# Softmax attention with a gated feed-forward on one core: down weights loaded earlier, splits moved and spread, other copied scores

## The chip, the cores and the metric

The kernel runs on one core of a Trainium2 chip. The metric is the device time of one execution, in microseconds (us). The engines named below are TensorE (PE in the profile, its weight loads PEld), VectorE (DVE), ScalarE (ACT), GpSimd (POOL) and SyncE (SP), which issues most of the DMAs from one queue, in order. A bank is one bank of TensorE's accumulation memory, 128 partitions by 512 numbers.

## The reference

Sequence 2048, width 512, all in float32. Cut to what matters:

```
xn = layernorm(x)
q, k, v = split(xn @ wqkv), 32 heads of 16
p = softmax(q @ k^T * 16**-0.5)            # per head, 2048 x 2048
s = (p @ v) @ wo
ffn = (silu(xn @ w_gate) * (xn @ w_up)) @ w_down     # inner width 1792
out = x + s * silu(ffn)
```

## The kernel before

**Precision.** A product that must be near float32 is made of three: operands are split into a high part in a rounded format and a low part (value minus high part), and high by high, high by low and low by high are summed. A split is therefore two DVE instructions, a copy that rounds (CAST in the profile) and a subtraction.

**Opening.** The first 160 us normalise x, project it to q, k and v, and write these to DRAM in the layout that the attention reads. The feed-forward's first gate/up tile is computed there too.

**Attention.** Heads go in 8 groups of 4, queries in 4 batches of 512: 32 units. A unit runs over 16 key tiles of 128. They are cut into blocks (L461 to L475), usually 5, 5 and 6 key tiles; units 27, 29 and 30 have 4 blocks of 4, unit 28 has 6, 6, 4 and unit 31 has 4, 3, 3, 3, 3. There are 101 blocks; `now` is the number of the one being written, and blocks are numbered so below, from 0. For each key tile there are two pairs of heads. A pair's scores take two matmuls of 50 rows that share the array, one per half.

**A block** (`run`, L852) has two stages. In the first, scores and steps of the feed-forward are written in turn; a step (`fill(1)`) is two matmuls of 64 rows (`both`, L184) that share the array and add into the banks `bankx` and `banky`. In the second stage (`values`, L371) TensorE multiplies the block's probabilities by v, 8 matmuls a key tile. TensorE works strictly in the written order.

**Direct and copied scores.** A direct pair ("D") goes into one of two score buffers, and ACT takes the exponential from there (L884), about one microsecond a pair; TensorE can be at most two pairs ahead of ACT. A copied pair goes by halves ("A", then "B") through one spare bank, `acc[1]`; DVE copies each half to SBUF (L896, L902), and ACT takes the exponential of copied pairs at the end of the stage (L908), while TensorE does values. B may be written only when A's copy has been read out. Copied pairs are always the block's last ones. `events` (L477) decides how many pairs are copied and at which step each D, A, B and F (a feed-forward step) stands: `need` is the number of pairs that ACT couldn't take directly in the stage's length, counted in steps; the number copied is that or a limit by length, whichever is less. In the first block nothing is copied, and four of its steps are written ahead of its scores (L855 and following).

**Feed-forward** (`ffn`, L195). Four batches of 512 rows; inner width 1792 is 14 tiles, in two groups of 7. A tile's gate and up products are 24 steps (gate in `bankx`, up in `banky`); then ACT takes a tanh of `bankx`, and DVE makes the hidden values `ga` in two instructions that read both banks (L218, L219). After 7 tiles come four down products of 21 steps, one for each 128 rows. A block takes exactly one of these, 24 or 21 steps; the last ones take the output projection, 9 or 12 steps (`project_out`, L338). "(6,21)" below means a block of 6 key tiles and 21 steps.

**Loads and splits of weights.** `load_gu` (L121) loads a gate/up tile two tiles ahead (`gur`, two buffers), `split_gu` puts its split into `chores`. `load_wd` (L146) loads a tile's down weights into `wdr`, which has one buffer, so that load waits for the split of the tile before; before the change it is issued after the 8th of the tile's 24 products, behind `load_gu`. `split_wd` (L151) puts its split among the chores after the 22nd. `split_hidden` splits `ga` into `hh`.

**Chores.** DVE's splits and the ends of units (`normalise`, `finish`) are kept in a list and written between the copies, where their cost in steps fits before the next copy; `tidy` (L139) writes all that is left, once ahead of the stage's last event and once behind it. DVE executes in that order, so that an instruction that waits holds all behind it. The steps and costs are numbers in the kernel; no scheduler changes the order.

**Output projection.** In the last blocks attention outputs of batches 0 to 2 are loaded from DRAM (`load_out`, L288) and split (`split_out`, L305): all three of a batch at the end of one block (L325). `ready` counts a batch's parts; its projection begins when it has four. `store_out` (L333) multiplies and adds on GpSimd.

Of the kernel before, what the change touches and what calls it, by code (L numbers as in the profile page):

```python
# [28 lines left out]
DT = D // P  # L29
# [21 lines left out]
def tile_block(ctx: ExitStack, tc: tile.TileContext, x, wqkv, wo, w_gate, w_up, w_down, out):  # L51
# [143 lines left out]
    def ffn(b):  # L195
        for grp, part in enumerate(GROUPS):
            nf = part.stop - part.start
            for f in range(nf):
                i = b * NF + part.start + f
                if i + 1 < NB * NF:  # L200
                    split_gu(i + 1)
                if i + 2 < NB * NF:
                    load_gu(i + 2)
                hi, lo = gu.pop(i)
                n = 0
                for c in range(DC):
                    for wt, j in ((hi, 0), (hi, 1), (lo, 0)):
                        both(wt[:, c], fx[:, j, c], n == 0, n == 3 * DC - 1)
                        n += 1
                        if n == 3 * DC - 2 and now >= 0:  # L210
                            split_wd(f, i)
                        if n == DC and i:
                            load_wd(i)
                        if n == 3 * DC:
                            th = one.tile([P, TB], F32, tag="th", name="th")
                            ga = two.tile([P, TB], F32, tag="ga", name="ga")
                            act(th, bankx, AF.Tanh, scale=0.5)  # L217
                            dve.scalar_tensor_tensor(ga, th, 1.0, bankx, op0=ALU.add, op1=ALU.mult)  # L218
                            dve.scalar_tensor_tensor(ga, ga, 0.5, banky, op0=ALU.mult, op1=ALU.mult)  # L219
                            kept.append((f, ga))  # L220
                            if now >= 0:
                                split_hidden()
                            if grp == 1 and f == nf - 1 and b + 1 < NB:
                                load_fx(b + 1, 0)
                                load_fx(b + 1, 1)
                            elif grp == 1 and f == nf - 1:
                                load_wo(0)
                        yield 3 * DC - n
            for t in range(NT):
                n = 0  # L230
                for f in range(nf):
                    for a, w in ((0, 0), (0, 1), (1, 0)):
                        both(hh[:, f, a, t * P:(t + 1) * P], wd[:, f, w], n == 0, n == 3 * nf - 1)
                        n += 1
                        if n == 3 * nf and grp == 0:
                            dve.tensor_copy(facc[:, t], bankx)
                            dve.tensor_add(facc[:, t], banky, facc[:, t])
                        elif n == 3 * nf:
                            y = two.tile([P, D], F32, tag="ga", name="y")
                            dve.tensor_add(y, bankx, facc[:, t])  # L240
                            dve.tensor_add(y, banky, y)
                            after.append(partial(store_gate, y, b * TB + t * P))
                            if b == NB - 1:
                                after.append(partial(next_out, t))
                        yield 3 * nf - n
# [56 lines left out]

    ready = [0] * NB

    def split_out(b):  # L305
        for c in range(DT - 1):
            split_o(lhs[b, c], parts_o[b, c])
            ready[b] += 1

    def out_steps():  # L310
        if now == early:
# [11 lines left out]
            load_gate()  # L323

    def out_splits():  # L325
        if now in (early, early + 1):
            split_out(now - early)
        if now == opened[units - 2] + 1:
            split_out(2)
        if now - opened[units - 1] - 2 in range(EARLY):  # L330
            gate_rest(now - opened[units - 1] - 2)

# [127 lines left out]
    for u in range(units):  # L460
        opened.append(len(blocks))  # L461
        if u == units - 1:
            ns = [4, 3, 3, 3, 3]
        elif u in FINE:
            ns = [4] * 4
        elif u == units - 4:
            ns = [6, 6, 4]
        else:
            ns = [5] * 3
            far = sizes[len(blocks):len(blocks) + 3]  # L470
            ns[far.index(max(far)) if far[1] < max(far) else 1] = 6
        kt = 0
        for n in ns:
            blocks.append((u, kt, n))
            kt += n  # L475

    def events(n, f):  # L477
        length = 2 * n + f
        need = 2 * n - max(2, (10 * length + 46) // 40)
        copied = max(0, min(need, (2 * length - 5) // 22)) if now else 0  # L480
        direct = 2 * n - copied
        gap = max(4, min(5, (length - 8) / max(1, direct - 2)))
        marks = [(0, "D"), (1, "D")] + [(7 + gap * i, "D") for i in range(direct - 2)]
        marks += [(3 + max(5.6, (length - 5) / (2 * copied)) * i, "AB"[i % 2]) for i in range(2 * copied)]
        marks.sort()
        out = []
        at = left = 0
# [426 lines left out]
    for now, (u, first, n) in enumerate(blocks):  # L914
        g, b = divmod(u, NB)
        if first == 0 and 0 < u < units - 1:
            load_q(u + 1)
            load_shift(u + 1)
        if now == 2 or first == 0 and 0 < g < NG - 1 and b == 0:
            load_k(g + 1, 0)  # L920
            load_v(g + 1, 0)
        run(u, first, n)
# [93 lines left out]
```

## Time and profile before

| | us |
|---|---|
| median of 3 runs | 1434.6 (1433.69 to 1435.59) |
| the profiled execution, its own time | 1435.62 |
| its span on the core | 1433.8 |
| TensorE busy | 1409.6 (98%) |
| ScalarE busy | 1080.5 (75%) |
| VectorE busy | 734.7 (51%) |
| GpSimd busy | 89.9 (6%) |
| mean granted TensorE clock | 0.996 |

How to read it: a busy TensorE is one with a matmul in flight, and matmuls overlap, so 98% says that it seldom stands still, and not that nothing can be shortened. The chain of waits follows the work that ended last back through the program; its rows name a line, a start and a duration. In it "PE acc L375" is a run of value matmuls (x40 for a block of 5 key tiles, x48 for 6, x32 for 4, x24 for 3), so that the distance from the end of one such row to the end of the next is the length of a block. A wait is put down to the instruction that ended it.

### The profile page before, as it was taken

How to read it: one execution, taken by the hardware profiler on the slowest of the kernel's cores; microseconds unless marked ns; L12 is line 12 of the kernel's file. 1: busy time of each engine (PE TensorE's matmuls, PEld its weight loads, DVE VectorE, ACT ScalarE, POOL GpSimd, SP SyncE). 2: the span in 40 equal slices, each digit the busy share in tenths (PEclk: the TensorE clock that was granted, in tenths of full speed). 3: DMA queues.
4: the chain of work that ended last, by engine and by line, in shares of the span. 5: the costliest groups of instructions: out<-in, count | busy, mean ns of one | idle time of the engine just before them, and what ended most of it. 6: DMA issues, size and time to landing. Idle time of an engine off the chain costs nothing.

```text
span 1433.8 us, 27758 instructions
## 1 busy us (share of the span) xinstructions
PE 1409.6 (98%) x11227; PEld 860.7 (60%) x11227; DVE 734.7 (51%) x1251; ACT 1080.5 (75%) x1235; POOL 89.9 (6%) x104
## 2 busy tenths in 40 slices
PE   9999899999999999999999999999999999999998
PEld 7777565566555655566556556665566556554445
DVE  6543355356545553556455535554555355445446
ACT  6733577787788777787888778878887778687775
POOL 4200200000000000000000000000000000001333
PEclk9999999999999999999999999999999999999999
DMA  6768642034543511154514303365224112133323
GB/s 221 264 244 252 165 103 50 13 88 95 115 108 97 134 42 35 47 125 101 134 54 114 83 12 79 82 149 123 71 73 115 35 44 67 59 111 108 115 88 119
DMA packets 126956, 148.17 MB, mean 103 GB/s; under 512 B 12524, under 2 KB 79340, under 8 KB 126052
## 3 DMA queue, kind: packets, MB, share of 16 engines
q1 hardware_dynamic: 121620, 125.79, 34.3%
q0 software_dynamic: 4912, 20.12, 3.8%
q8 instruction: 91, 1.49, 0.4%
q14 instruction: 45, 0.37, 0.1%
q10 hardware_dynamic: 288, 0.39, 0.1%
HBM read 106.68 MB, written 39.58 MB: 102 GB/s over the span
## 4 chain that ended last, share of the span: by engine, by line
PE 91%; ACT 4%; DVE 2%; DMA 1%; issue 1%; SPq 0%; DVEq 0%; ACTq 0%
PE acc L375 30%; PE bankx L186 23%; PE score L868 15%; PE banky L186 9%; PE ps L622 6%; ACT pr L884 4%; PE ps L624 3%; PE acc L868 3%; DMA wdr<-in_B_w_down_dram 1%; PE acc L597 0%; DMA v_d<-vt 0%; DMA wraw<-in_A_wqkv_dram 0%; DVE hh L276 0%; PE ps L653 0%; SPq L98 0%
## 5 line engine op out<-in xcount | busy, mean ns | idle before, releaser
L884 ACT ACTIVATE pr<-score 128x1024 f32<-128x1024 f32 x876 | 823.9, 1030 | 260.5 <-PE score L868 260.0
L375 PE MATMUL acc<-pr,vst 128*17 128x512 f32 x4096 | 460.9, 595 | 0.0
L868 PE MATMUL score<-qst,kst 50*128 50x512 f32 x1752 | 412.1, 420 | 10.8 <-ACT pr L884 10.5
L186 PE MATMUL bankx<-fx,guh 64*128 64x512 f32 x896 | 320.2, 394 | 3.3 <-DVE ga L218 3.2
L186 PE MATMUL banky<-fx,guh 64*128 64x512 f32 x896 | 312.3, 395 | 0.6 <-DVE ga L219 0.6
L375 PEld LDWEIGHTS acc<-pr,vst 128*17 128x17 f32 x4096 | 110.3, 97 | 294.7 <-issue 287.8
L868 PEld LDWEIGHTS score<-qst,kst 50*128 50x128 f32 x1752 | 177.3, 184 | 169.9 <-issue 74.8
L186 PE MATMUL bankx<-wd,hh 64*128 64x512 f32 x672 | 199.2, 392 | 0.0
L186 PE MATMUL banky<-wd,hh 64*128 64x512 f32 x672 | 196.6, 391 | 0.0
L896 DVE COPY pr<-acc 128x512 f32<-128x512 f32 x148 | 102.2, 690 | 176.7 <-PE acc L868 173.7
L186 PEld LDWEIGHTS bankx<-fx,guh 64*128 64x128 f32 x896 | 167.2, 187 | 19.7 <-DVE ga L218 4.0
L186 PE MATMUL bankx<-fx,gul 64*128 64x512 f32 x448 | 176.4, 394 | 0.0
L186 PE MATMUL banky<-fx,gul 64*128 64x512 f32 x448 | 176.2, 393 | 0.0
L186 PEld LDWEIGHTS banky<-fx,guh 64*128 64x128 f32 x896 | 167.2, 187 | 6.2 <-DVE ga L219 1.4
L902 DVE COPY pr<-acc 128x512 f32<-128x512 f32 x148 | 102.2, 691 | 102.5 <-PE acc L868 92.1
L908 ACT ACTIVATE pr<-pr 128x1024 f32<-128x1024 f32 x148 | 153.5, 1083 | 0.0
L186 PEld LDWEIGHTS bankx<-wd,hh 64*128 64x128 f32 x672 | 125.1, 186 | 13.1
L186 PEld LDWEIGHTS banky<-wd,hh 64*128 64x128 f32 x672 | 124.9, 186 | 4.4
L868 PE MATMUL acc<-qst,kst 50*128 50x512 f32 x296 | 118.1, 399 | 1.6 <-DVE pr L896 1.5
L218 DVE SCALAR_TENSOR_TENSOR ga<-th,bankx 128x512 f32<-128x512 f32 x56 | 38.5, 687 | 137.9 <-ACT th L217 137.9
L186 PEld LDWEIGHTS bankx<-fx,gul 64*128 64x128 f32 x448 | 84.3, 188 | 6.9
L186 PEld LDWEIGHTS banky<-fx,gul 64*128 64x128 f32 x448 | 84.1, 188 | 1.6
(171 smaller groups left out, 1302.8 us busy)
## 6 DMA issues: line engine op xcount, KB each, us to landing
gur<-in_B_w_gate_dram SPq DMA_DIRECT2D x56, 256.0 KB
gur<-in_B_w_up_dram SPq DMA_DIRECT2D x56, 256.0 KB
wdr<-in_B_w_down_dram SPq DMA_DIRECT2D x56, 256.0 KB
kst<-k_d SPq DMA_DIRECT2D x192, 64.0 KB
qst<-q_d SPq DMA_DIRECT2D x192, 64.0 KB
fx<-xt_d SPq DMA_DIRECT2D x24, 512.0 KB
q_d<-parts SPq DMA_DIRECT2D x16, 512.0 KB
k_d<-parts SPq DMA_DIRECT2D x16, 512.0 KB
```

Source lines behind the costliest of these rows:

```text
L186: mm(banks[i], lhs[halves[i]], rhs[halves[i]], start=start, stop=stop)
L218: dve.scalar_tensor_tensor(ga, th, 1.0, bankx, op0=ALU.add, op1=ALU.mult)
L375: mm(acc[0][h * 32:h * 32 + DH + 1], v[:, kt % CT, h * (DH + 1):(h + 1) * (DH + 1)], probs[kt, h // 2][:, h % 2], start=kt == 0, stop=kt = ...
L622: mm(ps, w, a[:, c], start=n == 0, stop=n == 3 * DT - 1)
L624: mm(ps, a[:, c, tokens], w, start=n == 0, stop=n == 3 * DT - 1)
L868: mm(bank, k[r, j, kc * P:(kc + 1) * P], q[r, j], start=True, stop=True)
L884: act(probs[kt, j], score[done % 2], AF.Exp, scale=0.25)
L896: dve.tensor_copy(probs[kt, j][:, 0], spare_bank)
L902: dve.tensor_copy(probs[kt, j][:, 1], spare_bank)
L908: act(probs[kt, j], probs[kt, j], AF.Exp, scale=0.25)
```

## The change

Five things are changed.

1. A tile's down weights are loaded at its first product, ahead of `load_gu`, instead of after its 8th.
2. In block 0 the split of the down weights is written behind the two instructions that read the banks, instead of ahead of them.
3. The splits of batches 0 to 2 for the output projection are spread: blocks 87, 88 and 89 end with two each (before: three after 87, three after 88), and blocks 93, 94 and 95 with one each (before: three after 93).
4. Unit 0 is cut into blocks of 4, 6 and 6 key tiles instead of 5, 6 and 5, and the load of the second group's first keys and values moves from block 2 to block 3.
5. The limit on copied pairs is another formula, and copies are placed otherwise. Written out, 162 pairs are copied instead of 148: a third pair in the seven blocks (6,21), which are 7, 19, 40, 52, 73, 85 and 86; a second pair in six of the blocks with 4 key tiles and 12 steps, which are 89, 90, 91, 93, 94 and 95; and one more in block 2, which now has 6 key tiles. Elsewhere the number stays. A and B of a pair are at most 8 steps apart by the formula (before: spread over the stage): in the 29 blocks of 5 key tiles and 24 steps B now stands 10.5 steps into the stage.

The order of one (6,21) block and of one (4,12) block, before and after:

```
(6,21)  DDFAFFFFDFFBDFFFDFAFFDFFFDBFFDFFDDF   ->  DDFAFFFFDBFFDFFAFDFFFBDFFDFAFFDFFBDF
(4,12)  DDFAFFFFDFFBDFFFDFDDF                 ->  DDFAFFFFDBFFDFFAFDFBDF
```

The diff:

```diff
@@ ffn @@
             for f in range(nf):
                 i = b * NF + part.start + f
+                if i:
+                    load_wd(i)
                 if i + 1 < NB * NF:
                     split_gu(i + 1)
...
-                        if n == 3 * DC - 2 and now >= 0:
+                        if n == 3 * DC - 2 and now > 0:
                             split_wd(f, i)
-                        if n == DC and i:
-                            load_wd(i)
                         if n == 3 * DC:
...
                             kept.append((f, ga))
+                            if now == 0:
+                                split_wd(f, i)
                             if now >= 0:
                                 split_hidden()
@@ split_out, out_splits @@
-    def split_out(b):
-        for c in range(DT - 1):
-            split_o(lhs[b, c], parts_o[b, c])
-            ready[b] += 1
+    def split_out(b, c):
+        split_o(lhs[b, c], parts_o[b, c])
+        ready[b] += 1
...
-        if now in (early, early + 1):
-            split_out(now - early)
-        if now == opened[units - 2] + 1:
-            split_out(2)
+        for b, c in {early: ((0, 0), (0, 1)), early + 1: ((0, 2), (1, 0)), early + 2: ((1, 1), (1, 2)),
+                     opened[units - 2] + 1: ((2, 0),), opened[units - 2] + 2: ((2, 1),),
+                     opened[units - 2] + 3: ((2, 2),)}.get(now, ()):
+            split_out(b, c)
@@ blocks @@
             ns = [4, 3, 3, 3, 3]
+        elif u == 0:
+            ns = [4, 6, 6]
@@ events @@
-        copied = max(0, min(need, (2 * length - 5) // 22)) if now else 0
+        fit = 1 if ends and length < 24 else (10 * length + 34) // 112
+        copied = max(0, min(need, fit)) if now else 0
...
-        marks += [(3 + max(5.6, (length - 5) / (2 * copied)) * i, "AB"[i % 2]) for i in range(2 * copied)]
+        marks += [(2.2 + max(5.6, min(8, (length - 5) / (2 * copied))) * i, "AB"[i % 2]) for i in range(2 * copied)]
@@ the loop over blocks @@
-        if now == 2 or first == 0 and 0 < g < NG - 1 and b == 0:
+        if now == 3 or first == 0 and 0 < g < NG - 1 and b == 0:
             load_k(g + 1, 0)
             load_v(g + 1, 0)
```

## The prediction, made before the result was known

> **What bounds the kernel.** I read the page first, then the chain of waits, then the timeline where the chain leaves TensorE.
>
> ```profile
> span 1433.8 us, 27758 instructions
> ...
> PE 91%; ACT 4%; DVE 2%; DMA 1%; issue 1%; SPq 0%; DVEq 0%; ACTq 0%
> ...
> L868 PE MATMUL acc<-qst,kst 50*128 50x512 f32 x296 | 118.1, 399 | 1.6 <-DVE pr L896 1.5
> ```
>
> TensorE carries 91% of the chain, so no edit here shortens its work (the products are the same before and after). What can move is the other 9%: stretches where TensorE waits for a score buffer (ACT), for copies or splits (DVE), or for weights (DMA), and the half-clock stretches that such waits bring. A block is one stage of scores and one of values (program order, from 0). Its length is the distance between two ends of value stages, start plus duration in the chain's rows (start, duration, what):
>
> ```profile
> 83.17 22.39 PE ps L622 x96
> ...
> 657.81 5.28 PE acc L375 x48
> ...
> 683.16 4.42 PE acc L375 x40
> 691.78 0.96 ACT pr L884
> ...
> 696.46 5.27 PE acc L375 x48
> 709.22 4.42 PE acc L375 x40
> 721.14 4.42 PE acc L375 x40
> 734.46 5.28 PE acc L375 x48
> ```
>
> One step (a product, or a pair that shares the array) takes 22.39/96 = 0.233 us; one key tile more costs 5.27 - 4.42 = 0.85 us of values. Block 40 has 6 key tiles and 21 feed-forward steps, (6,21): 701.73 - 687.58 = 14.15; block 41, (5,21), takes 11.91, and block 43, (6,24), 739.74 - 725.56 = 14.18. The odd one is (6,21): three steps fewer than (6,24), the same time. The row at 691.78 says why: ten scores go straight to ACT, and TensorE waits for ACT's pitch.
>
> **The change, part by part.**
>
> *A third copied pair in the seven (6,21) blocks.* Nine direct scores remain. Without the wait a block takes between 11.91 + 0.85 + 2 x 0.233 = 13.23 and 14.18 - 3 x 0.233 = 13.48: a gain of 0.67 to 0.92 us. The cost: two copies more on DVE, 0.69 us each (rows of L896 below), and six half scores through one bank, 5.5 steps = 1.28 us apart, against 0.40 (the half score of the group above) + 0.69 + two hand-overs, estimated at 1.2 us. That just fits, so I take 0.75. Below nothing: if each of the six is 0.2 us late, the gain is gone. ACT does the same number of exponentials, the third copied one beside the 5.3 us of values as the other two now. Six of the seven: 4.5 us. Block 85 starts behind a DVE backlog, and its second half score now comes two steps earlier against the same late copy: 0.2 us. Together 4.7.
>
> *A second copied pair in six of the 12-step blocks (89, 90, 91, 93, 94, 95), splits of the output projection spread.*
>
> ```profile
> 1287.61 5.27 PE acc L375 x48
> ...
> 1309.17 4.92 PE acc L375 x32
> ...
> 1320.14 3.56 PE acc L375 x32
> ...
> 1360.46 1.66 DVE hh L276
> ...
> 1369.58 3.56 PE acc L375 x32
> ...
> 1404.37 2.82 PE acc L375 x24
> 1411.66 2.80 PE acc L375 x24
> ```
>
> Block 89 takes 1323.70 - 1314.09 = 9.6. Block 99 (3 key tiles, 12 steps, one pair copied, no wait for ACT) takes 7.27; one key tile more makes 8.59, so at most 1.01 is to be had. But the written order puts the second pair's halves only 3.5 steps = 0.82 us apart, against the 1.2 above: about 0.35 lost. 0.66 each, for five blocks 3.3. Block 90 gets nothing: two splits of batch 1 now end block 89, where GpSimd starts on the gated output; the split at 1360.46 stood in such a place and took 1.66 us, and two like it would hold the first copy of block 90 by about 0.8 us. In block 94 it is the three splits of batch 2, now one per block, that held the first copy, to 1365.27:
>
> ```profile
> 1365.27 0.68 DVE L896 COPY pr<-acc 128x512 f32<-128x512 f32 x1
> ```
>
> Blocks 93 and 94 together took 1373.14 less 1348.92 + 3.56 (the row of block 92, below), 20.66: 1.5 over two of 9.6. This goes too. Sum 4.8 (bounds 2 and 6.5).
>
> *The splits of batch 0, three after block 87 before, two now.* Blocks 87 and 88 take 1314.09 - 1292.88 = 21.21, 2.0 over twice 9.6. Value stage 88 took 4.92 instead of 3.56 at half clock, which followed a stretch in which TensorE was only 72% busy:
>
> ```profile
> 1348.92 3.56 PE acc L375 x32
> ...
> 1304.00:1308.50 4.50, 3.24 (x22) 1.90 (x20) 3.80 (x8) 4.19 (x6) 0.00 (x0) 1.00 0.98 313
> 1308.50:1311.90 3.40, 3.40 (x20) 0.66 (x20) 2.56 (x5) 2.40 (x3) 0.00 (x0) 0.50 1.04 386
> ```
>
> (columns: stretch, length, then busy of PE, PEld, DVE, ACT and POOL, granted clock, DMA share, GB/s). The rest of the 2.0, 0.65, is a first copy held by the splits, and goes with one split fewer; the 1.36 of half clock goes in perhaps 7 of 10 cases, since block 88 stays bound by ACT. I take 1.6 (0.3 to 2.0).
>
> *Down weights at a tile's first product.* SyncE's queue runs in order; the load moves ahead of the two gate/up loads (gur) of 256 KB each. It still waits for the split of the last tile's weights, and now the gur loads wait behind that: they have a whole block, over 11 us, before their split. Where key rows are loaded, the down weights came too late:
>
> ```profile
> 475.73 4.42 PE acc L375 x40
> ...
> 501.97 5.27 PE acc L375 x48
> ...
> 631.40 4.42 PE acc L375 x40
> ...
> 747.90 4.42 PE acc L375 x40
> ...
> 773.83 5.27 PE acc L375 x48
> 787.32 4.42 PE acc L375 x40
> 796.84 6.70 DMA wdr<-in_B_w_down_dram
> 814.84 5.27 PE acc L375 x48
> ```
>
> A (5,24) and a (6,24) block undisturbed take 779.10 - 752.32 = 26.78 (blocks 45, 46). 48 and 49 take 28.37, 24 and 25 take 27.09, 36 and 37 (to 663.09) 27.27: 1.59, 0.31 and 0.49 over, 2.4. The load comes about 1.3 us earlier and without 512 KB ahead of it, some 3 us in all: it does for nearly all. I take 2.2 (1.5 to 2.4).
>
> *The opening: units of 4, 6, 6 key tiles and the split behind the bank reads.*
>
> ```profile
> 169.98 1.29 DVE L906 TENSOR_TENSOR gul<-gur,guh 128x512 fp32r<-128x512 f32 x2
> 170.13 0.66 SPq L125 DMA_DIRECT2D gur<-in_B_w_gate_dram  x1
> 171.58 0.55 SPq L148 DMA_DIRECT2D wdr<-in_B_w_down_dram  x1
> 176.39 0.43 DVE L906 CAST wd<-wdr 128x512 fp32r<-128x512 f32 x1 [5.12 <-DMA wdr<-in_B_w_down_dram]
> 178.20 0.50 PE L186 MATMUL bankx<-fx,guh 64*128 64x512 f32 x1 [2.82 <-DVE ga L218]
> 178.97 0.43 DVE L906 CAST hh<-ga 128x512 fp32r<-128x512 f32 x1
> 180.64 0.68 DVE L896 COPY pr<-acc 128x512 f32<-128x512 f32 x1
> ...
> 178.70:185.50 6.80, 6.51 (x30) 5.42 (x31) 4.45 (x8) 2.05 (x2) 0.00 (x0) 0.50 0.83 183
> ...
> 203.90 4.42 PE acc L375 x40
> ```
>
> Before: DVE waits for the weights, the reads of the banks queue behind, TensorE stands for 2.82 us and then runs 6.8 us at half clock. After: block 0 begins near 160.2 as before; 8 scores and 24 products are 32 steps, 7.45 us, the values begin near 168.0 and end at 171.6. DVE ends its gate split at 171.27, reads the banks by 172.7 (0.3 us of waiting for TensorE), then waits for the weights. Issued at 170.13 they are there between 173.1 (3 us) and 174.9 (the 4.8 us of before); I take 174.1. The wait is thus not gone: behind it stand the weight split (1.07), the hidden split and the gate cast (178.97 to 180.64, 1.67) and the first copy, which ends at 177.5. TensorE wants that bank again 10.5 steps into block 1, at 174.7: it stands 2.9 us there. I add one half-clock period of 3.4 us, 1.7 lost. Block 1: 0.35 + 36 x 0.233 + 0.2 + 0.3 + 2.9 + 1.7 = 13.8, and 5.3 of values: 190.7. Block 2, now (6,24), ends at 204.9, against 208.32: gain 3.4 (1.0 with late weights and two periods, 6 with early weights and none).
>
> In this case half clock followed a stretch without any long pause (1304 to 1308.5), so I count it after 2.9 us. The Trainium skill, "TensorE: Matmul & The Clock Gate", section "Why this matters for your kernels", says otherwise that only gaps of more than about 3 us between bursts bring half clock; the row at 1308.50 disagrees. By that rule the opening would gain 5.1 and the sum would be 1416.
>
> *Earlier second halves elsewhere* (29 blocks (5,24): 10.5 steps after the start instead of 18) cost nothing as long as DVE has done the first copy; see the last rival. K and V of the second group move a block later, needed nine blocks on: nothing.
>
> **Sum.** 4.7 + 4.8 + 1.6 + 2.2 + 3.4 = 16.7 us. The profiled execution took 1435.6 (span 1433.8 and 1.8 around it), 1.0 above the median of 1434.6; it becomes 1418.9, and the median 1417.9.
>
> **Rivals.** (a) No half clock in the opening: 1416. For it: 2.9 us may fall across two periods of observation; against it, the row at 1308.50. (b) The 13 extra pairs do not pay, because the shared bank's round trip of 1.2 us is longer than I read it: 4.5 and 3.3 fall away, 1425.7. For it: spacings of 1.28 and 0.82 us leave no room. Against it: the rows of copy and half score, 1.09 together. (c) The opening gains nothing, because the weights land late and both periods stay: 1421. (d) Slower: in the 29 (5,24) blocks TensorE comes to the second half before the first copy is done.
>
> ```profile
> 209.47 0.69 DVE L896 COPY pr<-acc 128x512 f32<-128x512 f32 x1
> ```
>
> Block 3 began at 208.32; the copy ended 1.84 us in, TensorE will come at 0.33 + 10.5 x 0.233 = 2.78. DVE would have to be 0.94 us later than here before anything is lost; at 0.58 us lost per block the whole gain is gone, at 0.75 the time is 1440.
>
> **How the numbers follow.** A measurement here tells about 0.2%, 2.9 us, from no change. Forecast 1418: 0.48; (a) 0.15; (b) 0.20; (c) 0.09; (d) 0.08, of which 0.03 within 0.2% and 0.05 slower. So faster 0.92, same 0.03, slower 0.05. The likeliest case alone spans 1413 to 1422; with (a), (b) and (c) the range is 1411 to 1427.
>
> **What would show it.** In the changed profile: (6,21) blocks of about 13.4 us; block 91 near 8.9; blocks 48 and 49 near 26.8 together; in the opening no wait for "ga", but one of the second half score (acc, L868 before) for DVE of 2 to 3 us; first three blocks over by 205. Wrong would be: waits of TensorE for the copies in block after block, or half clock at places that had none.

## The result, and the profile after

The changed kernel takes 1422.2 us (median of 4 runs, 1421.64 to 1426.21) against 1435.1 for the kernel before (4 runs): a ratio of 0.9916, 95% interval 0.9895 to 0.9937. That is 13 us less, where 16.7 were predicted; the time lies 4.2 us above the 1418.0 of the prediction, inside its range and just outside that of its likeliest case. The profiled executions differ by 14.0: 1435.62 before, 1421.64 after (span 1419.9).

From the page of the changed kernel, the span, the shares of the chain by engine, and the group of the half scores that share a bank (busy and mean ns, then the idle time ahead of them):

```profile
span 1419.9 us, 27729 instructions
...
PE 94%; DVE 2%; ACT 2%; DMA 1%; issue 1%; SPq 0%; DVEq 0%; ACTq 0%
...
L872 PE MATMUL acc<-qst,kst 50*128 50x512 f32 x324 | 130.5, 403 | 5.2 <-issue 2.5
```

TensorE carries 94% of the chain instead of 91, and ACT 2% instead of 4. There are 324 half scores instead of 296, and TensorE waits 5.2 us for their bank instead of 1.6; 2.5 of these are one wait in the opening. (The page puts that wait down to "issue", which means that it shows nothing that ended it; the rows of the opening below tell what did.) From the chain of waits of the changed kernel (start, duration, what):

```profile
184.95 5.28 PE acc L376 x48
199.11 5.28 PE acc L376 x48
...
676.64 4.42 PE acc L376 x40
689.11 5.27 PE acc L376 x48
...
780.06 4.42 PE acc L376 x40
...
806.00 5.27 PE acc L376 x48
...
1288.61 3.56 PE acc L376 x32
...
1298.22 3.56 PE acc L376 x32
...
1309.37 1.70 DVE wd L278
1311.07 1.44 DVE wd L277
...
1317.46 3.87 PE acc L376 x32
...
1326.90 3.87 PE acc L376 x32
```

As in the prediction, a block's length is the distance between two ends of value stages. Block 40, (6,21), takes 694.38 - 681.06 = 13.32 (before 14.15). Blocks 48 and 49 take 811.27 - 784.48 = 26.79 together (before 28.37). Block 88 takes 1301.78 - 1292.17 = 9.61 (before 11.62). But block 91, one of the six with a second copied pair, takes 1330.77 - 1321.33 = 9.44, and its value stage is longer, 3.87 instead of 3.56. The two rows of DVE in front are from the splits that end block 89: 1.70 and 1.44 us, and block 90 behind them comes to 10.1.

The table adds up all blocks in this way, profiled execution against profiled execution:

| Term of the sum | predicted | measured | blocks |
|---|---|---|---|
| third copied pair, (6,21) | 4.7 | 4.1 | 7, 19, 40, 52, 73: 0.66 to 0.84 each, 3.7; 85: 0.29; 86: 0.11 |
| second copied pair and spread splits, 12 steps | 4.8 | 1.7 | 89, 91, 93, 95: 0.12 to 0.17 each; 90: -0.52; 94: 1.64 |
| splits of batch 0 | 1.6 | 1.4 | 88: 2.01; 87: -0.61 |
| down weights, later blocks | 2.2 | 2.0 | 25: 0.32; 37: 0.16; 49: 1.55 |
| opening | 3.4 | 3.9 | end of block 2: 204.39, before 208.32 |
| the rest | 0 | 0.8 | 30, 31, 68, 80, 96: 0.18 to 0.29 each; 56: -0.25; the end behind the last block: -0.4 |
| sum | 16.7 | 13.9 | |

In the opening the timeline of the changed kernel shows these instructions (start, duration, engine, what, and in brackets the wait and what ended it):

```profile
174.14 0.43 DVE L910 CAST wd<-wdr 128x512 fp32r<-128x512 f32 x1 [0.68 <-DMA wdr<-in_B_w_down_dram]
...
177.22 0.69 DVE L910 CAST guh<-gur 128x1024 fp32r<-128x1024 f32 x1 [0.86 <-DMA gur<-in_B_w_up_dram]
177.83 0.68 DVE L900 COPY pr<-acc 128x512 f32<-128x512 f32 x1
...
178.61 0.46 PE L872 MATMUL acc<-qst,kst 50*128 50x512 f32 x1 [2.47 <-issue]
```

The weights are there at 174.1, as predicted. TensorE then stands for 2.47 us at the half score that wants the bank of the first copy, which starts at 177.83 and takes 0.68. The rows of these stretches by engine (stretch, length, busy of PE, PEld, DVE, ACT and POOL, granted clock, DMA share, GB/s) show what the wait did to the clock, which is nothing here (where the stretches begin and end is explained under "Half clock after a wait" below):

```profile
173.87:177.28 3.41, 2.24 (x16) 1.56 (x15) 2.21 (x5) 1.51 (x2) 0.00 (x0) 1.00 0.98 196
177.28:180.70 3.42, 2.09 (x18) 2.00 (x20) 3.12 (x5) 1.29 (x2) 0.00 (x0) 1.00 1.02 227
```

### The profile page after: what moved, and what is told of

The parts are those of the page before. It is cut to its first block, busy times and chain, and to the rows that moved or that the text cites. A ratio compares the mean times of both kernels' runs of the same rounds, so it can differ in the third digit from the quotient of the medians.

```text
span 1419.9 us, 27729 instructions
## 1 busy us (share of the span) xinstructions
PE 1403.0 (99%) x11227; PEld 847.5 (60%) x11227; DVE 756.3 (53%) x1279; ACT 1082.0 (76%) x1235; POOL 92.7 (7%) x104
## 4 chain that ended last, share of the span: by engine, by line
PE 94%; DVE 2%; ACT 2%; DMA 1%; issue 1%; SPq 0%; DVEq 0%; ACTq 0%
PE acc L376 30%; PE bankx L186 23%; PE score L872 16%; PE banky L186 10%; PE ps L626 6%; PE acc L872 3%; PE ps L628 3%; ACT pr L888 1%; DVE pr L900 0%; DMA v_d<-vt 0%; PE acc L601 0%; ACT pr L912 0%; DMA wraw<-in_A_wqkv_dram 0%; PE ps L657 0%; PE acc L957 0%
## 5 line engine op out<-in xcount | busy, mean ns | idle before, releaser
L888 ACT ACTIVATE pr<-score 128x1024 f32<-128x1024 f32 x862 | 812.0, 1033 | 244.5 <-PE score L872 243.2
L872 PE MATMUL score<-qst,kst 50*128 50x512 f32 x1724 | 396.1, 417 | 3.2 <-ACT pr L888 3.1
L186 PE MATMUL bankx<-fx,guh 64*128 64x512 f32 x896 | 331.5, 393 | 0.3 <-DVE ga L218 0.2
L186 PE MATMUL banky<-fx,guh 64*128 64x512 f32 x896 | 323.3, 393 | 0.3 <-DVE ga L219 0.3
L872 PEld LDWEIGHTS score<-qst,kst 50*128 50x128 f32 x1724 | 172.5, 184 | 158.6 <-issue 72.3
L900 DVE COPY pr<-acc 128x512 f32<-128x512 f32 x162 | 112.0, 691 | 171.6 <-PE acc L872 167.0
L186 PEld LDWEIGHTS bankx<-fx,guh 64*128 64x128 f32 x896 | 166.4, 186 | 19.9 <-issue 0.9
L912 ACT ACTIVATE pr<-pr 128x1024 f32<-128x1024 f32 x162 | 166.6, 1081 | 0.0
L906 DVE COPY pr<-acc 128x512 f32<-128x512 f32 x162 | 111.9, 691 | 88.4 <-PE acc L872 72.9
L872 PE MATMUL acc<-qst,kst 50*128 50x512 f32 x324 | 130.5, 403 | 5.2 <-issue 2.5
```

Source lines behind the costliest of these rows:

```text
L186: mm(banks[i], lhs[halves[i]], rhs[halves[i]], start=start, stop=stop)
L872: mm(bank, k[r, j, kc * P:(kc + 1) * P], q[r, j], start=True, stop=True)
L888: act(probs[kt, j], score[done % 2], AF.Exp, scale=0.25)
L900: dve.tensor_copy(probs[kt, j][:, 0], spare_bank)
L906: dve.tensor_copy(probs[kt, j][:, 1], spare_bank)
L912: act(probs[kt, j], probs[kt, j], AF.Exp, scale=0.25)
```

## The experiments

Twelve kernels were run. All edits are against the changed kernel, but for the one that starts from the kernel before. Ratios are to the kernel before on the same chip.

| Kernel | median us | ratio and interval |
|---|---|---|
| changed, run again | 1423.23 | 0.9916 (0.9902 to 0.9930) |
| loads late again | 1428.29 | 0.9940 (0.9919 to 0.9960) |
| two copied pairs in (6,21) | 1426.89 | 0.9930 (0.9910 to 0.9951) |
| one copied pair at 12 steps | 1423.81 | 0.9916 (0.9894 to 0.9937) |
| splits together again | 1423.93 | 0.9913 (0.9891 to 0.9934) |
| even distances at 12 steps | 1426.33 | 0.9926 (0.9908 to 0.9943) |
| one exponential left out | 1423.12 | 0.9900 (0.9868 to 0.9933) |
| opening as before, load early | 1420.34 | 0.9880 (0.9862 to 0.9898) |
| block 1's copies late | 1418.42 | 0.9872 (0.9855 to 0.9890) |
| kernel before, load early alone | 1427.96 | 0.9947 (0.9931 to 0.9964) |
| splits of 84 to 87 as chores | 1421.46 | 0.9901 (0.9883 to 0.9918) |
| the last two late edits together | 1415.73 | 0.9866 (0.9850 to 0.9882) |

Runs of the same opening differ by a stretch or two at half clock, each of 3.4 us, so a few tenths in a median decide nothing. The verdicts below rest on the lengths of blocks. Where the opening is the same, blocks that no edit and no half clock touches repeat to within 0.07 us; where an edit shifts all that follows (experiments 2, 7, 8, 9 and 11), a few blocks far from it move by 0.1 to 0.3 us (19, 37, 56 and 68 in experiment 9), which nothing here explains.

**1. The load of the down weights alone, undone.**

```diff
-                if i:
-                    load_wd(i)
...
+                        if n == DC and i:
+                            load_wd(i)
```

> The changed kernel with one part undone: the down weights are loaded after a tile's 8th product again, behind the gate/up loads. Theory: the part was worth what blocks 25, 37 and 49 lost less, 0.3 + 0.2 + 1.6 = 2.0 us, and in the opening the weights land at about 176.4 again instead of 174.1, so that the first copy of block 1 ends 1.0 to 2.3 us later: block 49 back near 15.7 us, the whole 3.0 to 4.3 us slower than the changed kernel. Rival: the load's place does nothing in the opening, because the gate/up tile that then lands earlier (it ended the last 0.9 us of that wait) takes its part: block 1 as in the changed kernel within 0.5 us, the whole 2.0 slower.

From the timeline and the chain of that run:

```profile
177.27 0.43 DVE L910 CAST wd<-wdr 128x512 fp32r<-128x512 f32 x1 [3.91 <-DMA wdr<-in_B_w_down_dram]
```

```profile
202.74 5.27 PE acc L376 x48
```

The weights come 3.1 us later than in the changed kernel (177.27 against 174.14), and block 2 ends at 208.01 instead of 204.39, of which a half-clock stretch at 180.5 is about 1.15. Blocks 25, 37 and 49 are 0.91, 1.06 and 1.16 longer, block 13 0.37. In 25 and 37 the late load costs more in this order than it cost before the change. In all the early load is worth about 6 us by these blocks (2.5 in block 2 without the half clock, 3.5 in the four others), more than both theories had expected. It is the largest part of the change, and more than the 2.2 us at which the prediction booked it; the rest it had booked under the opening.

**2. A third copied pair in (6,21), taken back.**

```diff
+        fit = min(fit, 2)
         copied = max(0, min(need, fit)) if now else 0
```

> The changed kernel with at most two copied pairs in a block, so that the seven (6,21) blocks copy two again. Theory: in blocks 7, 19, 40, 52 and 73 the third pair gained 0.7 to 0.8 us each, in 85 0.3, in 86 0.1, and it cost 0.6 in block 87, because the third copied exponential delays the tanh of the gate behind it, DVE's work that waits for the tanh, and so the next block's first copy. Then 7, 19, 40, 52, 73 return to 14.15, block 87 returns to 9.6, and the whole is 3.4 us slower. Rival: block 87 is slower because the second half of its copied pair stands a step earlier against a copy that is late anyway; then block 87 stays near 10.2 us and the whole is 4.0 us slower.

Blocks 7, 19, 40, 52 and 73 become longer by 0.66, 0.81, 0.81, 0.70 and 0.71: the 0.75 of the prediction. The chain at blocks 85 to 87 of that run:

```profile
1268.27 5.27 PE acc L376 x48
...
1282.42 5.28 PE acc L376 x48
...
1293.91 3.56 PE acc L376 x32
```

Block 86 takes 14.16 and block 87 9.77. In the changed kernel they take 14.03 and 10.21. So the third pair is worth 0.45 in block 85 and 0.12 in 86, and costs 0.43 in block 87: together 0.14. The rival, by which block 87 would have stayed near 10.2, is refuted.

**3. A second copied pair in the blocks of 12 steps, taken back.**

```diff
+        fit = 1 if length < 24 else fit
         copied = max(0, min(need, fit)) if now else 0
```

> The changed kernel with one copied pair in every block of 12 steps or fewer, as before the change. Theory: the second pair is worth next to nothing there, because ACT's eight exponentials follow one another without a break through both stages and the block ends when the last of them and its values are done: blocks 89, 91, 93, 94 and 95 go from 9.44 to 9.60, the whole is slower by 0.8 us at most. Rival: the second pair does remove a wait of 0.9 us and gives it back through its own late half; then without it too blocks are at 9.60, and the two theories part only in the order of the copies, which another run changes. Block 90, where DVE's splits meet GpSimd's product, stays above 9.6 by up to 0.5 us.

From the chain:

```profile
1318.93 3.56 PE acc L376 x32
...
1328.51 3.56 PE acc L376 x32
```

Block 91 takes 9.58 with one copied pair and 9.44 with two; 89, 93, 94 and 95 gain 0.12 to 0.17, and block 90 loses 0.13 by it. Value stages take 3.56 again. The six pairs are thus worth 0.75 - 0.13 = 0.6 in all, where the prediction had 3.3.

**4. One exponential fewer in those blocks.** In blocks 89, 90, 91, 93, 94 and 95 the exponential of the first copied pair is left out; the values are computed from what stands there.

```diff
-        for kt, j in waiting:
+        for kt, j in waiting[1:] if n == 4 and len(waiting) == 2 else waiting:
```

> The changed kernel without the exponential of the first copied pair in the six 12-step blocks with two such pairs (89, 90, 91, 93, 94, 95): the raw scores go on to the values there, so that part of the softmax is left out. Theory: ACT's row of exponentials sets the length, and with one fewer the value stage no longer waits: from 9.44 to about 9.1 us (3.6 of values and the 5.5 of the score stage), 2 us in all. Rival: the spacing of the halves alone makes the extra time and the value stage's extra 0.3 us come from the late last copy on DVE; then the blocks stay near 9.44.

ACT's rows in the timeline of block 91, first in the changed kernel:

```profile
1321.86 5.93 ACT L888 ACTIVATE pr<-score 128x1024 f32<-128x1024 f32 x6 [1.62 <-PE score L872]
...
1327.69 1.99 ACT L912 ACTIVATE pr<-pr 128x1024 f32<-128x1024 f32 x2
```

and then with one left out:

```profile
1321.89 5.91 ACT L888 ACTIVATE pr<-score 128x1024 f32<-128x1024 f32 x6 [2.25 <-PE score L872]
...
1327.70 1.05 ACT L912 ACTIVATE pr<-pr 128x1024 f32<-128x1024 f32 x1
```

In the changed kernel ACT's eight exponentials run without a break from 1321.86 to 1329.68, and the block that began at 1321.33 ends at 1330.77: 0.53 ahead of the row, 7.82 of exponentials, 1.09 of last products behind it. With two of the eight copied instead of one, ACT has the same eight to do. With one left out five of the six blocks become shorter by 0.30 to 0.35 (block 91: 9.10), and another limit comes next; block 90, which the splits hold, stays at 10.13. TensorE's rows of the same block, the two halves of the second copied pair:

```profile
1324.71 0.39 PE L872 MATMUL acc<-qst,kst 50*128 50x512 f32 x1
...
1325.95 0.50 PE L872 MATMUL acc<-qst,kst 50*128 50x512 f32 x1
```

They start 1.24 us apart where the order puts 3.5 steps, 0.82 us, between them: TensorE is held for 0.4. It is held as long in the changed kernel, hidden behind ACT.

**5. The halves of the short blocks closer to even, 4.8 apart by the formula.**

```diff
-        marks += [(2.2 + max(5.6, min(8, (length - 5) / (2 * copied))) * i, "AB"[i % 2]) for i in range(2 * copied)]
+        apart = 4.8 if length < 24 else max(5.6, min(8, (length - 5) / max(1, 2 * copied)))
+        marks += [(2.2 + apart * i, "AB"[i % 2]) for i in range(2 * copied)]
```

> The changed kernel with the copied halves of its short blocks (under 24 steps in all) 4.8 steps apart, so that the two pairs of the 12-step blocks stand 4.5 and 5.5 steps apart by halves instead of 5.5 and 3.5. Rival (the prediction's own): the 3.5 steps cost 0.35 to 0.5 us of TensorE's time a block; then blocks 89, 91, 93, 94 and 95 fall from 9.44 to about 9.1 us and the whole by 1.7 us or more. Theory: ACT's eight exponentials in a row set the length; then the score stage gets shorter, the value stage waits that much longer, and the blocks stay within 0.1 us of 9.44.

The row of ACT in the timeline of block 91 that begins with the third direct score:

```profile
1325.13 3.92 ACT L889 ACTIVATE pr<-score 128x1024 f32<-128x1024 f32 x4 [0.32 <-PE score L873]
```

The blocks became longer, 9.70. TensorE still waits at the second half, and now the third direct score comes late, so that ACT's row has a hole of 0.32: the length follows ACT (9.44 + 0.27). The theory that only the 3.5 steps between two halves hold the block is refuted, since it asked for a shorter one; the other, which asked for no change, missed the hole. Blocks with one copied pair became longer too: 97 to 100 by 0.41 each, 87, 88, 92 and 96 by 0.33 to 0.42. There A and B came closer as well, to 4.5 steps (1.05 us), and B now stands ahead of the third direct score instead of behind it. In block 97 the two halves, and ACT's row from that third score on:

```profile
1381.88 0.39 PE L873 MATMUL acc<-qst,kst 50*128 50x512 f32 x1
...
1383.12 0.50 PE L873 MATMUL acc<-qst,kst 50*128 50x512 f32 x1
...
1383.94 2.85 ACT L889 ACTIVATE pr<-score 128x1024 f32<-128x1024 f32 x3 [0.33 <-PE score L873]
```

The halves start 1.24 us apart, as in experiment 4, and the third direct score waits behind the second half, so that ACT's row has a hole of 0.33; in the changed kernel the five direct exponentials of such a block run without a break. So this is the same loss as in block 91: a score that ACT needs stands behind a half that is held. The hold alone, 1.24 - 4.5 x 0.233 = 0.19, is less than half of the 0.41. The 5.5 steps (1.28 us) of the (6,21) blocks are just enough by the same number.

**6. The splits of a batch together again.**

```diff
-        for b, c in {early: ((0, 0), (0, 1)), early + 1: ((0, 2), (1, 0)), early + 2: ((1, 1), (1, 2)),
-                     opened[units - 2] + 1: ((2, 0),), opened[units - 2] + 2: ((2, 1),),
-                     opened[units - 2] + 3: ((2, 2),)}.get(now, ()):
+        for b, c in {early: ((0, 0), (0, 1), (0, 2)), early + 1: ((1, 0), (1, 1), (1, 2)),
+                     opened[units - 2] + 1: ((2, 0), (2, 1), (2, 2))}.get(now, ()):
```

> The changed kernel with the splits of the output projection as before, three at the end of blocks 87, 88 and 93. Theory: what the spreading moved is undone: block 94 1.5 us longer (near 10.9), block 88 0.65 us longer (near 10.3, and 1.4 more where half clock follows), block 90 0.5 us shorter (near 9.6), the whole 1.7 to 3.0 us slower. Rival: block 94 gained because of its second copied pair and not by the splits; then it stays within 0.3 us of 9.44, and the whole is within 1 us of the changed kernel.

The chain of that run, blocks 92 and 94 and between them the split that holds:

```profile
1337.89 3.56 PE acc L375 x32
...
1349.05 1.66 DVE hh L278
1350.70 1.44 DVE hh L277
...
1358.17 3.87 PE acc L375 x32
```

Blocks 93 and 94 take 20.59, against 18.86 in the changed kernel: the spread is worth 1.7 there, as booked (1.5). Block 88 is 0.64 longer, also as booked (0.65). Block 90 is 0.68 shorter (9.44): the two splits that end block 89 in the changed kernel cost this much, and nothing forces them to stand there.

**7. The opening as before, with the early load kept** (units of 5, 6, 5; the split ahead of the bank reads; keys and values at block 2).

```diff
-        elif u == 0:
-            ns = [4, 6, 6]
...
-                        if n == 3 * DC - 2 and now > 0:
+                        if n == 3 * DC - 2 and now >= 0:
...
-                            if now == 0:
-                                split_wd(f, i)
...
-        if now == 3 or first == 0 and 0 < g < NG - 1 and b == 0:
+        if now == 2 or first == 0 and 0 < g < NG - 1 and b == 0:
```

> The changed kernel with its opening undone (unit 0 in blocks of 5, 6, 5; keys of the second group after block 2; the down weights' split ahead of the bank reads in block 0), but with the down weights still loaded at the first product. Theory: the early load alone did the opening's work; the weights land at about 174.1, DVE reads the banks by 176.7, TensorE stands about 1.2 us there and 0.4 us at the first copy, and block 2 ends near 203 us, 1.4 to 2.5 us ahead of the changed kernel. Rival (the prediction's step): the new order and the smaller first block carry the opening's gain; then block 2 ends near 208 and the whole is 3 to 4 us slower.

From its chain:

```profile
170.59 6.18 PE acc L374 x40
...
185.67 5.27 PE acc L374 x48
199.14 4.42 PE acc L374 x40
```

Block 2 ends at 203.56, 0.83 earlier than in the changed kernel (less than the 1.4 to 2.5 expected), though this run has a half-clock stretch there (at 170.9, granted clock 0.51 from 170.90 to 174.30) and the changed one has none. Block 1 has no wait (14.17).

**8. The early load alone, in the kernel before.** The same move of `load_wd` to the first product, and nothing else.

> The kernel before with one part of the change alone: the down weights loaded at a tile's first product. Theory: this part carries the whole gain of the opening and of the loads between groups: block 2 ends near 202 us (203.6 with a half-clock period) instead of 208.3, blocks 24 and 25, 36 and 37, 48 and 49 take 26.8 us by pairs, and the whole is 7 to 8.5 us faster than the kernel before. Rival: in the opening the early load helps only together with the split behind the bank reads; then block 2 ends near 206 or later and the gain is 2 to 4 us.

From its chain, the value stage of block 2:

```profile
198.79 4.42 PE acc L375 x40
```

One moved load takes 7.7 us (1435.65 to 1427.96): block 2 ends at 203.21 instead of 208.32, and blocks 25, 37 and 49 gain 0.29, 0.48 and 1.59. So the changed kernel's new order of the opening, with the same load, ends 1.2 us later than the old order does.

**9. Block 1's copies later.** The copies of block 1 begin at step 16, and DVE's other work of that block stands behind them.

```diff
-        marks += [(2.2 + max(5.6, min(8, (length - 5) / (2 * copied))) * i, "AB"[i % 2]) for i in range(2 * copied)]
+        start, apart = (16, 5.6) if now == 1 else (2.2, max(5.6, min(8, (length - 5) / max(1, 2 * copied))))
+        marks += [(start + apart * i, "AB"[i % 2]) for i in range(2 * copied)]
...
-            while chores and at < final and (not copying or max(free, t) + chores[0][0] <= copying[0] + 0.5):
+            while chores and at < final and (now != 1 or not copying) and (not copying or max(free, t) + chores[0][0] <= copying[0] + 0.5):
```

> The changed kernel with the two copied pairs of block 1 moved back, the first half to step 16 instead of 3, and DVE's other work of that block behind the copies. Theory: TensorE's 2.7 us wait in block 1 is for the bank whose copy stands behind the waits for the down and gate weights, and half clock follows it by chance of the observation period; with the copies late the wait goes, block 1 falls from 18.3 (19.5 with half clock) to about 15.3 us, the whole is 3.0 us faster, and no run has half clock in the opening. Rival: the wait only moves to the next tile's gate weights, whose split now comes later; then block 2 is longer by what block 1 gains.

From its chain:

```profile
181.35 5.28 PE acc L376 x48
195.51 5.27 PE acc L376 x48
```

Block 1 takes 14.82 instead of 18.32, block 2 is not longer (14.15), and block 2 ends at 200.78. The whole wait of 2.47 us was the place of the first copy in the order, and it does not come back in block 2, as the rival had it; no half clock follows in the profiled run either. Block 1 gains 1.0 more than the wait; DVE's other work was moved too, and the two were not separated.

**10. The splits of blocks 84 to 87 among the chores.** They are no longer written at a block's end, ahead of the next one's first copy, but among the chores, and in blocks 85 to 87 no chore is written ahead of the first copy (`held`).

```diff
-        if t:
-            split_o(lhs[NB - 1, t - 1], plain[t - 1])
-        split_wo(t)
+        chores.append((2, lambda: dve.tensor_copy(fx[:, 0, t], wor[t])))
+        chores.append((3, lambda: dve.tensor_sub(fx[:, 1, t], wor[t], fx[:, 0, t].bitcast(F32))))
...
+            for c in range(DT - 1):
+                hi, lo = lhs[NB - 1, c]
+                chores.append((2, partial(dve.tensor_copy, hi, plain[c])))
+                chores.append((3, partial(dve.tensor_sub, lo, plain[c], hi.bitcast(F32))))
...
+        held = len(copying) if u == units - 4 else -1
...
-            while chores and at < final and (not copying or max(free, t) + chores[0][0] <= copying[0] + 0.5):
+            while chores and at < final and len(copying) != held and (not copying or max(free, t) + chores[0][0] <= copying[0] + 0.5):
```

> The changed kernel with the splits of the last batch's outputs and of the projection's weights (next_out) written among the chores, the outputs' already in block 84, and in blocks 85 to 87 nothing of the chores ahead of the first copy. Theory: the third pair earns little in 85 and 86 and costs in 87 because DVE stands behind the tanh with this work when the first copy is due; without it blocks 85 and 86 fall from 14.46 and 14.03 to 13.3 to 13.5 us and 87 from 10.20 to 9.6, 2.2 us in all. Rival: these blocks are long by ACT alone, which has the tanh besides its exponentials there; then they stay within 0.3 us each.

DVE's rows at the end of block 85 in the changed kernel:

```profile
1267.08 0.69 DVE L191 SCALAR_TENSOR_TENSOR y<-th,y 128x512 f32<-128x512 f32 x1 [2.75 <-ACT th L190]
...
1269.20 0.69 DVE L258 TENSOR_TENSOR fx<-wor,fx 128x512 fp32r<-128x512 f32 x1
1269.81 0.68 DVE L900 COPY pr<-acc 128x512 f32<-128x512 f32 x1
```

The gate's tanh stands behind the copied exponentials on ACT, and with a third of these it comes later; the splits wait behind it, and the first copy of block 86, which began at 1267.93, starts at 1269.81. With the splits among the chores blocks 85, 86 and 87 gain 1.10, 0.67 and 0.60 (13.35, 13.36 and 9.60).

**11. Experiments 9 and 10 together, with one more split moved** from the end of block 89 to that of block 90:

```diff
-        for b, c in {early: ((0, 0), (0, 1)), early + 1: ((0, 2), (1, 0)), early + 2: ((1, 1), (1, 2)),
+        for b, c in {early: ((0, 0), (0, 1)), early + 1: ((0, 2), (1, 0)), early + 2: ((1, 1),), early + 3: ((1, 2),),
```

> The two mendings together, late copies in block 1 and the splits of next_out among the chores, and one split a block in blocks 89 and 90. Theory: the gains add up, 3.5 us in the opening (more where half clock was), 2.2 in blocks 85 to 87 and 0.5 in block 90: 6 us less than the changed kernel, about 1416 where that takes 1422, and no half clock before the end. Rival: work pushed behind the copies comes back as longer blocks later, and the gain is under 4 us.

From its page and chain:

```profile
span 1413.5 us, 27726 instructions
...
PE 96%; ACT 1%; DVE 1%; DMA 1%; issue 0%; SPq 0%; DVEq 0%; ACTq 0%
...
181.40 5.28 PE acc L379 x48
```

1415.7 us (four runs, 1415.27 to 1417.15): 7.5 less than the changed kernel run again, 19.9 less than the kernel before. Block 90 takes 9.44, block 1 14.82, block 85 13.31.

**12. The changed kernel again.**

> The changed kernel itself once more beside the others. Theory: its runs fall into some with half clock in the opening and some without, about 1.2 us apart, by where the observation period lies against the wait of 2.7 us; the granted clock tells them apart. Rival: the spread has another source, and runs of equal clock differ by as much.

Six runs gave 1421.69 to 1428.88, a wider spread than the 1.2 us expected; the two longest, 1425.98 and 1428.88, have the lowest mean clocks, 0.996 and 0.995. In the profiled one, which is the longest, block 1 takes 21.01 instead of 18.32, and two of the stretches by engine are at half clock (a third lies at 10.0 us, long before the attention):

```profile
180.70:187.50 6.80, 6.37 (x30) 5.49 (x32) 2.90 (x5) 3.07 (x3) 0.00 (x0) 0.50 0.98 187
1293.40:1296.80 3.40, 3.22 (x16) 1.00 (x20) 1.83 (x4) 3.01 (x4) 0.00 (x0) 0.50 0.26 60
```

The same program has no such stretch in the profile of the result above, with a wait of 2.47 us where this run has 2.61. Block 87 took 11.67 here, 10.21 there.

## Why the prediction was right, and where it was off

**The third copied pair (4.7, measured 4.1): right.** 0.66 to 0.84 in the five blocks that begin undisturbed, against 0.75, and experiment 2 takes exactly this back. The reading of the odd row, ten direct scores at ACT's pitch, was the right one. Block 86 was counted with the undisturbed ones and is not: it stands, like 85, behind DVE's splits.

**The second copied pair at 12 steps (3.3 of the 4.8, measured 0.6): this term was mis-sized, and it is nearly all of what is missing.** The step that failed is the sentence "one key tile more makes 8.59, so at most 1.01 is to be had". It scaled a block with six exponentials up to one with eight by TensorE's time alone, and booked nothing for ACT. Experiment 4 shows what sets the length: ACT does eight exponentials in 7.82 us without a break, and copying a pair moves its exponential to the end of the row without taking it away. Copying helps a block in which ACT has time left during the values, as in (6,21) (six key tiles' values, 5.3 us), and not one in which it has none. The time of the prediction's rival (b) nearly came true for these six pairs, though not for its reason: the round trip of the shared bank does hold TensorE, as experiment 4 shows, but behind ACT.

**The spread splits (1.5 in block 94, 0.65 in 88): right,** 1.64 and, from experiment 6, 0.64. Block 90 was booked as "gets nothing", with 0.8 of cost set against the second pair's gain; the cost was there (0.68) and the gain wasn't, so the block lost 0.52.

**Splits of batch 0 (1.6, measured 1.4): right in sum, by parts that were not foreseen.** Block 88 gained all of the 2.0, half clock included, but the 1.36 of this is in part luck: the profiled run has no half clock in these blocks, while in experiments 7 and 12 block 87 has a stretch of it. And block 87 lost 0.61. The third copied exponential of block 86 delays the gate's tanh, DVE's splits wait for it, and block 87's first copy waits for them. "The third one beside the 5.3 us of values" was true for TensorE, and not for what else stands on ACT. Experiment 2 prices this at 0.43, experiment 10 shows that the splits' place decides it.

**Down weights (2.2, measured 2.0): right** in the later blocks. It was the larger part of the opening's term too: experiment 8 gives 7.7 us for the load alone.

**The opening (3.4, measured 3.9): right, with two errors that cancel.** Weights at 174.14 (174.1 predicted), a wait of 2.47 us (2.9), block 2 over at 204.4 (204.9). Not foreseen was that behind the splits DVE would wait 0.86 us more for the gate/up tile, whose load now stands behind the down weights in SyncE's queue; and the half-clock stretch that I had added for certain did not come in this run. That it did not come is luck: of the eight profiles with this opening (the result's and those of experiments 2 to 6, 10 and 12) five have it, at 178 to 181. In experiments 2, 3 and 6 one stretch cost 1.15 us and not 1.7 (block 1, 19.45 to 19.51 against 18.32). The signs promised (no wait for "ga", a wait of 2 to 3 us at the second half score) are there. What the prediction did not ask was whether the new order is better than the old one once the load is early. It isn't: experiments 7 and 8 end block 2 earlier with the old order.

**Rivals.** (a), no half clock in the opening, is what the profiled run shows, and its time of 1416 was missed because of the 12-step blocks. (c) gives a time as near as any, 1421, but its reason is wrong: the weights came early and the opening gained 3.9. (d), slower (5,24) blocks, did not come: 48 and 49, a (5,24) and a (6,24) block, take 26.79, as undisturbed ones did before (26.78).

**Half clock after a wait.** The prediction counted one after a wait of 2.9 us, against the rule of the Trainium skill ("TensorE: Matmul & The Clock Gate", section "Why this matters for your kernels") that has no idle gaps above about 3 us between matmul bursts. The result's profile agrees with that rule, with 2.47 us and no half clock. Other runs show that keeping to it is not enough. From experiment 3, the wait in the timeline and the stretches by engine around it:

```profile
177.79 0.47 PE L873 MATMUL acc<-qst,kst 50*128 50x512 f32 x1 [2.14 <-issue]
```

```profile
175.60:179.00 3.40, 1.26 (x11) 1.16 (x12) 2.75 (x6) 1.05 (x2) 0.00 (x0) 1.00 0.86 212
179.00:182.40 3.40, 3.40 (x18) 3.05 (x17) 1.28 (x2) 2.53 (x3) 0.00 (x0) 0.50 1.10 208
```

In the profiles that have several, half-clock stretches start a whole number of 3.413 us apart (9.99, 180.66 and 1293.40 in experiment 12: 50 and 376 such lengths), so that the time between them can be cut in the same places. Cut so, the wait of 2.14 us fell into one stretch, which leaves it 1.26 busy, and the next runs at half clock. In the profile of the result a longer wait, 2.47 us, stands across the border of two stretches that are 2.24 and 2.09 busy, and the clock stays full. So the length of the wait alone does not decide. But the busy share of a stretch does not settle it either. The stretch ahead of the half clock at 1308.5 in the kernel before:

```profile
1305.08:1308.49 3.41, 2.22 (x13) 1.35 (x15) 2.75 (x5) 3.10 (x4) 0.00 (x0) 1.00 1.01 335
```

It is 2.22 busy, more than the 2.09 that nothing followed, and no pause in it is longer than 0.71 us. Of the stretches at full clock in the fourteen profiles, from 165 to 1400 us, half clock followed all seven that are at most 1.4 us busy, none that is more than 2.35, and five of the eighteen between. What does part them is the number of matmuls that start in the stretch: at most 13 where half clock followed, at least 14 in all others. This was read off afterwards, some records can be missing, and no run tried it, so the cause stays open.

## What to carry to other kernels

Moving work from one place on an engine to another gains only where that engine has time left: add up all of an engine's work in the block, end to end, before taking a lighter block as the yardstick. A queue that runs in order is cheap to mend by putting the late load first, and that was the largest part here; but a reordering made for a late load should be asked again once the load is early. What stood in the order directly ahead of a short hand-over (a copy that frees a bank) cost its whole duration here, and whatever it waited for.

## What was not expected of the hardware

- Half-clock stretches come in pieces of 3.4 us (3.4 and 6.8 in the rows above) and change from run to run of one program. The Trainium skill, "TensorE: Matmul & The Clock Gate", section "What's actually happening", gives a free-running window of 3413 ns; the lengths agree. A stretch costs less than half of itself: block 1 lost 1.15 us, block 87 1.46, presumably since part of it lies beside waits.
- A split's subtraction and the next one's rounding copy take 1.70 and 1.44 us at 1309.37 and 1311.07, while GpSimd multiplies and adds for the gated output, against 0.69 (L258 in experiment 10) and 0.43 (the rows of L910 in the opening) elsewhere. The prediction had this from a row of the kernel before.
- The two halves of a copied pair start 1.24 us apart where the order asks for less: for 0.82 us in experiment 4, for 1.05 in experiment 5. What such a hold costs depends on what the order puts behind it: nothing where ACT is behind anyway, more than itself where a direct score for ACT waits there.
